# A channel-attention kernel: part of x kept on the chip in 12 bits an element

## The chip, the cores and the metric

The kernel runs on one core of one Trainium2 chip. The metric is the device time of a launch in microseconds (us): the median of several executions. One execution was also taken by the hardware profiler; its span, from the first to the last instruction, is what the views of the profile divide up.

## The reference

x is 384 x 384 pixels by 384 channels in bf16 (147,456 pixels, 113.2 MB). For each channel the mean and the maximum over all pixels are computed, both go through the same small two-layer network, and a sigmoid of the sum scales the channel:

```python
B, H, W, C = x.shape
xf = x.reshape(B, H * W, C)
gap = jnp.mean(xf, 1)
gmp = jnp.amax(xf, 1)
h_a = gap @ w1
h_a = h_a * (h_a > 0)
h_m = gmp @ w1
h_m = h_m * (h_m > 0)
scale = _sigmoid(h_a @ w2 + h_m @ w2)
return x * scale[:, None, None, :]
```

The elements of x are normal numbers times 0.05 in bf16. No output can be written before all of x was read once, and x is far larger than the memory on the chip.

## The kernel before, in words

The pixels are cut into 1152 "rows": a row is 128 pixels, one on each partition, times 384 channels, 98,304 bytes in all. A block of n rows gives each partition n neighbouring pixels, so a transfer of a block has one run of n x 768 bytes for each partition. Six slots of 44 rows (`SLOTS`), a buffer `held` of 21 rows and an accumulator `acc` of 11 rows lie in SBUF; 16 + 2 rows are kept in PSUM (`kept_ps`, `kept_b`).

**Pass 1** goes over the list `loads` (lines 137 to 207). Each load is issued from SP's queue (line 184). TensorE sums its rows over the partitions with matmuls by a vector of ones (`sums`, line 157; four rows at a time, and the three groups of 128 channels write to partitions 0, 32 and 64 of one PSUM bank); the last loads are summed by `tail_sums` (line 174). VectorE keeps the running maximum in `acc` (line 200), in instructions over 6 and 5 rows in turn. The first 16 + 2 rows are copied to PSUM (lines 205 and 207). A load into a slot waits until VectorE and TensorE have done with what lay there. The blocks of `PASSING` go through the slots and are forgotten; those of `STAYING` come last and stay.

**The turn** (lines 210 to 241): `turn_sums` and `tail_sums` end the means, the 11 rows of `acc` are folded to one, three transposes and reductions end the maxima, and small matmuls and a sigmoid give `scale_bc`, the scale on all partitions. The 11 rows that `acc` displaced are read again.

**Pass 2** multiplies on VectorE (line 246) and stores from ACT's queue (line 264). `put` multiplies and stores a block in pieces, `get` reads a block again into a slot whose last store has landed (SP's queue, line 273). The order of SP is the order written in the loop; `FIRST_STORES` and `FIRST_READS` cut the first blocks in pieces, and the first two slots are read into after both were put (`LEAD`). 838 rows are read again (`AGAIN`). At the end come `held` and the rows kept in PSUM, which are multiplied into a slot:

```python
    while k < len(order):
        put(order[k], stores.pop(0) if stores else (order[k][1],), None if k else ACC_STORES_AT)
        k += 1
        if k == LEAD:
            for j in range(k):
                read_into(order[j][2])
        elif k > LEAD:
            read_into(order[k - 1][2])
```

Tile, the layer below, sets the semaphores by the regions that instructions read and write, and orders the engines by its own plan except where `manual_schedule` names an engine.

Of the kernel before, what the change touches and what calls it, by code (L numbers as in the profile page):

```python
# [13 lines left out]
U32 = mybir.dt.uint32  # L14


SLOTS = (44, 44, 44, 44, 44, 44)
PSUM_ROWS = 16
RING_BYTES = 256
HELD_ROWS = 21  # L20
BANK_ROWS = 2

FIRST_LOAD = 4
ACC_PARTS = ((0, 6), (6, 11))
ACC_ROWS = 11

PASSING = (
    43, 44, 44, 43, 43, 44, 43, 42, 42, 39, 38, 37, 36, 36, 35, 34, 32, 29, 29, 27, 27, 23, 15, 13,
)
STAYING = (  # L30
    (19, 17, 8), (18, 16, 10), (16, 14, 14), (13, 11, 11, 9), (10, 9, 9, 8, 8), (6, 6, 5, 5, 5, 4, 4, 3, 3, 3),
)

AGAIN = (44,) * 18 + (23, 23)

FIRST_STORES = ((1, 2, 3, 4, 4, 6, 8, 8, 8), (8, 8, 9, 9, 10), (10, 12, 22))

FIRST_READS = ((8, 8, 8, 10, 10), (44,))
LEAD = 2

ACC_STORES_AT = 3
SUM_TAIL = 4
# [4 lines left out]
def kernel(  # L47
# [15 lines left out]
    NS = len(SLOTS)  # L63
# [5 lines left out]
    def rows_of(ap, first, n):  # L69

        return ap[first * P:(first + n) * P, :].rearrange("(p n) c -> p n c", n=n)
# [4 lines left out]


    beside = BANK_ROWS + A
    held_at = PSUM_ROWS + beside
    head = held_at + HELD_ROWS  # L80
    n_stay = sum(SLOTS)
    n_pass = TOT - head - n_stay
    assert sum(PASSING) == n_pass
    stay = []
    for i, n in enumerate(SLOTS):
        stay.append([head + n_pass + sum(SLOTS[:i]), n, i])
    assert sum(AGAIN) == n_pass
    again = [(head + sum(AGAIN[:i]), n) for i, n in enumerate(AGAIN)]

# [8 lines left out]
    NQP = (CQ - 1) * QP + 1  # L98
    pick = small[0:NQP, 10:10 + 2 * CQ].bitcast(F32)
    nc.vector.memset(pick, 0.0)  # L100
    for q in range(CQ):
# [12 lines left out]
    acc = consts.tile([P, A, C], BF16)  # L114
    nc.dynamic_dma_scratch_size = RING_BYTES
    nc.lookup_mloc("DynamicDMAScratchLoc").dims = [P, RING_BYTES]
    held = nc.alloc_sbuf_tensor_at("held", [P, HELD_ROWS, C], BF16, offset=RING_BYTES).ap()
    slots = [xpool.tile([P, n, C], BF16, name=f"x{s}") for s, n in enumerate(SLOTS)]

# [4 lines left out]
    sum_ps = bank_a[0:NQP, 0:MM_ROWS * P]  # L124
    nc.vector.memset(bank_a, 0.0)
    tp_ps = [
# [10 lines left out]

    bufs = [*slots, held]
    loads = [
        (0, PSUM_ROWS, NS - 2, 0, PSUM_ROWS), (PSUM_ROWS, beside, NS - 1, 0, beside), (held_at, HELD_ROWS, NS, 0, HELD_ROWS),  # L140
    ]
    done = head
    for i, n in enumerate(PASSING):
        loads.append((done, n, (i - len(PASSING)) % NS, 0, n))
        done += n
    for (first, n, s), pieces in zip(stay, STAYING):
        assert sum(pieces) == n
        for j, m in enumerate(pieces):
            loads.append((first, n, s, sum(pieces[:j]), sum(pieces[:j + 1])))
    n_loads = len(loads)  # L150
    tail_rows = sum(hi - lo for *_, lo, hi in loads[n_loads - SUM_TAIL:])
# [13 lines left out]
    def turn_sums():  # L165

        for r in range(MM_ROWS):
            nc.scalar.copy(out=s_sb[r % 2], in_=sum_ps[:, r * P:(r + 1) * P])  # L168
            nc.tensor.matmul(gsum_ps, lhsT=s_sb[r % 2], rhs=pick, start=(r == 0), stop=False)  # L169
# [9 lines left out]
    done = turn = 0  # L179
    for i, (first, n, s, lo, hi) in enumerate(loads):  # L180
        rows = bufs[s][:, lo:hi, :]
        m = hi - lo
        for a, b in ((0, FIRST_LOAD), (FIRST_LOAD, m)) if i == 0 else ((0, m),):
            nc.sync.dma_start(out=rows[:, a:b, :], in_=rows_of(xr, first, n)[:, lo + a:lo + b, :])  # L184
        if i < n_loads - SUM_TAIL:
            sums(rows, m, done, TOT - tail_rows)
        else:
            tail_sums(rows, m, i == n_loads - 1)
        done += m
        if i == n_loads - SUM_TAIL - 1:  # L190
            turn_sums()
        if i == 0:
            nc.vector.tensor_copy(out=acc, in_=rows[:, 0:A, :])  # L193
            lo = A
        j = 0 if i else A
        while j < m:
            c, e = ACC_PARTS[turn]
            turn = (turn + 1) % len(ACC_PARTS)
            e = min(e, c + m - j)
            nc.vector.tensor_tensor(  # L200
                out=acc[:, c:e, :], in0=acc[:, c:e, :], in1=rows[:, j:j + e - c, :], op=ALU.max
            )
            j += e - c
        if i == 0:
            nc.vector.tensor_copy(out=kept_ps.bitcast(U32), in_=rows.bitcast(U32))  # L205
        elif i == 1:
            nc.vector.tensor_copy(out=kept_b.bitcast(U32), in_=rows[:, 0:BANK_ROWS, :].bitcast(U32))

# [7 lines left out]
    def acc_rows(ap, lo, hi):  # L216
        return rows_of(ap, PSUM_ROWS, beside)[:, BANK_ROWS + lo:BANK_ROWS + hi, :]

    n = A
    acc_pieces = []  # L220
    while n > 1:
        h = n // 2
        nc.vector.tensor_tensor(out=acc[:, 0:h, :], in0=acc[:, 0:h, :], in1=acc[:, n - h:n, :], op=ALU.max)  # L223
# [4 lines left out]
        nc.sync.dma_start(out=acc[:, lo:hi, :], in_=acc_rows(xr, lo, hi))  # L228
        acc_pieces.append((lo, hi))
    for q0, part in tp_ps:  # L230
        n = part.shape[1]
        for q in range(q0, q0 + n):
            nc.tensor.transpose(out=part[:, q - q0, :], in_=acc[:, 0, q * P:(q + 1) * P], identity=ident_bf)  # L233
        nc.vector.tensor_reduce(out=gT[:, q0:q0 + n, 1], in_=part, axis=AX.X, op=ALU.max)  # L234
# [105 lines left out]
```

## Time and profile before

| | |
|---|---|
| median of 3 runs | 737.08 us (736.64 to 741.11) |
| profiled execution: time, span | 737.92 us, 736.1 us |
| TensorE busy, mean granted clock | 128.1 us (17%), 0.554 |
| VectorE busy | 490.2 us (67%) |
| ScalarE, GpSimd busy | 3.3 us, 0.7 us |
| moved | 310.26 MB: 196.85 read, 113.25 written; 421 GB/s over the span |
| first load issued, first multiply of pass 2, last multiply | 0.7, 275.8, 697.9 us |

In the views, PE is TensorE's matmuls and PEld its weight loads, DVE is VectorE, ACT ScalarE, SP the engine that issues the loads. The slices cut the span in 40 parts and give the busy share of each engine in tenths, and the rate of the transfers. A line of the groups names the line of the kernel, the engine, the operation and the shapes, then the busy time of the group, the mean time of one in ns, and the idle time in front of them with what ended it.

### The profile page before, as it was taken

What the parts mean: (1) busy time and instruction counts of PE and PEld (TensorE: products, weight loads), DVE (VectorE), ACT (ScalarE), POOL (GpSimd) and SP (SyncE); (2) the same over time, 40 slices, a digit from 0 to 9 for tenths busy, and PEclk for the clock granted to TensorE, in tenths of its full rate; (3) what the DMA queues carried; (4) which work ended last, traced back from release to release, by engine and by line L of the source; (5) the groups of instructions that cost most, each with busy time, mean ns of one, the idle gap of its engine ahead of it and who ended that gap; (6) DMA issues with size and microseconds to landing.
All of it is one profiled execution on the core that took longest, in us unless ns stands there. A gap on an engine that the chain in (4) does not pass through costs nothing.

```text
span 736.1 us, 2598 instructions
## 1 busy us (share of the span) xinstructions
PE 128.1 (17%) x969; PEld 41.1 (6%) x969; DVE 490.2 (67%) x286; ACT 3.3 (0%) x9; POOL 0.7 (0%) x6
## 2 busy tenths in 40 slices
PE   3334454454544550000000000000000000000000
PEld 0111111111111120000000000000000000000000
DVE  6789999999999989999444464444444444445400
ACT  0000000000000000000000000000000000000000
POOL 0000000000000000000000000000000000000000
PEclk9856667655556555555555555555555555555555
DMA  9999999999999979999999999999999999999998
GB/s 382 438 431 435 423 433 423 431 426 431 423 427 418 417 277 370 415 423 438 425 435 439 432 428 435 437 433 428 435 437 433 428 435 437 433 424 436 436 428 346
DMA packets 18956, 310.26 MB, mean 421 GB/s; under 512 B 2464, under 2 KB 3072, under 8 KB 8320
## 3 DMA queue, kind: packets, MB, share of 16 engines
q1 hardware_dynamic: 12464, 196.86, 63.0%
q10 hardware_dynamic: 6480, 113.25, 36.1%
q8 instruction: 7, 0.11, 0.1%
q14 instruction: 5, 0.04, 0.0%
HBM read 196.85 MB, written 113.25 MB: 421 GB/s over the span
## 4 chain that ended last, share of the span: by engine, by line
another core or an unknown queue 39%; DMA 39%; DVE 13%; DVEq 1%; SPq 1%; issue 1%; PE 0%; ACT 0%; ACTq 0%
DMA x<-in_x_dram 32%; DVE acc L200 10%; DMA out_dram<-x 7%; DVE x L246 2%; DVEq L335 1%; SPq L273 1%; SPq L184 0%; DVE acc L223 0%; DVE acc L246 0%; PE bank_a L240 0%; ACT scale_bc L241 0%; DVE small L234 0%; PE bank_a L233 0%; PE bank_a L238 0%
## 5 line engine op out<-in xcount | busy, mean ns | idle before, releaser
L246 DVE TENSOR_TENSOR x<-x,scale_bc 128x16896 bf16<-128x16896 bf16 (+11 forms) x40 | 224.9, 5665 | 188.6 <-DMA x<-in_x_dram 187.4
L200 DVE TENSOR_TENSOR acc<-acc,x 128x2304 bf16<-128x2304 bf16 (+5 forms) x221 | 241.4, 1167 | 12.6 <-DMA x<-in_x_dram 12.3
L157 PE MATMUL bank_a<-x,small 128*1 128x512 bf16 (+3 forms) x894 | 120.9, 571 | 140.4 <-DMA x<-in_x_dram 140.4
L157 PEld LDWEIGHTS <-small 128*1 128x1 bf16 x912 | 37.1, 110 | 229.2 <-issue 226.5
L193 DVE COPY acc<-x 128x4224 bf16<-128x4224 bf16 x1 | 1.3, 1260 | 5.2 <-DMA x<-in_x_dram 5.2
L200 DVE TENSOR_TENSOR acc<-acc,held 128x2304 bf16<-128x2304 bf16 (+2 forms) x4 | 4.6, 1201 | 0.0
L246 DVE TENSOR_TENSOR held<-held,scale_bc 128x8064 bf16<-128x8064 bf16 x1 | 4.4, 4351 | 0.0
L205 DVE COPY kept_ps<-x 128x3072 uint32<-128x3072 uint32 x1 | 3.4, 3355 | 0.0
L246 DVE TENSOR_TENSOR x<-kept_ps,scale_bc 128x6144 bf16<-128x6144 bf16 x1 | 3.4, 3350 | 0.0
L157 PE MATMUL bank_a<-held,small 128*1 128x512 bf16 (+1 forms) x18 | 2.4, 570 | 3.2 <-DMA held<-in_x_dram 3.2
L223 DVE TENSOR_TENSOR acc<-acc 128x384 bf16<-128x384 bf16 (+2 forms) x4 | 2.6, 658 | 0.1
L246 DVE TENSOR_TENSOR acc<-acc,scale_bc 128x1920 bf16<-128x1920 bf16 (+1 forms) x2 | 2.4, 1252 | 0.0
L168 ACT COPY w_sb<-bank_a 65x128 f32<-65x128 f32 x2 | 0.5, 262 | 265.2 <-PE bank_a L157 264.7
L174 PEld LDWEIGHTS <-x 128*128 128x128 bf16 x39 | 1.3, 109 | 0.0
L113 ACT ACT_TABLE_LOAD x1 | 1.3, 1283 | 0.7 <-PEq L324 0.7
L169 PE MATMUL bank_b<-small,w_sb 65*128 65x3 f32 x4 | 1.2, 365 | 0.4 <-ACT w_sb L168 0.4
L174 PE MATMUL bank_b<-small,x 128*128 128x1 bf16 x39 | 1.2, 165 | 0.0
L169 PE MATMUL bank_b<-small,scale_bc 65*128 65x3 f32 x4 | 1.1, 353 | 0.0
L169 PEld LDWEIGHTS bank_b<-small,w_sb 65*128 65x128 f32 x4 | 1.0, 313 | 0.9 <-ACT w_sb L168 0.9
L169 PEld LDWEIGHTS bank_b<-small,scale_bc 65*128 65x128 f32 x4 | 1.1, 323 | 0.0
L234 DVE TENSOR_REDUCE small<-bank_a 128x2 bf16<-128x256 bf16 x1 | 0.4, 427 | 0.6 <-PE bank_b L233 0.6
L233 PE MATMUL bank_a<-ident_bf,acc 128*128 128x128 bf16 x2 | 0.4, 301 | 1.9 <-DVE acc L223 1.9
(27 smaller groups left out, 7.5 us busy)
## 6 DMA issues: line engine op xcount, KB each, us to landing
out_dram<-x ACTq DMA_DIRECT2D x21, 4224.0 KB, 79.7
x<-in_x_dram SPq DMA_DIRECT2D x20, 4224.0 KB, 27.7
x<-in_x_dram SPq DMA_DIRECT2D x4, 4128.0 KB, 51.6
x<-in_x_dram SPq DMA_DIRECT2D x2, 4032.0 KB, 50.0
x<-in_x_dram SPq DMA_DIRECT2D x2, 3456.0 KB, 44.1
x<-in_x_dram SPq DMA_DIRECT2D x3, 2208.0 KB, 23.0
x<-in_x_dram SPq DMA_DIRECT2D x2, 2784.0 KB, 38.1
x<-in_x_dram SPq DMA_DIRECT2D x2, 2592.0 KB, 35.5
```

Source lines behind the costliest of these rows:

```text
L113: nc.scalar.activation(out=scale_bc[0:1, 0:1], in_=pick[0:1, 0:1], func=ACT.Sigmoid)
L157: nc.tensor.matmul(sum_ps[q * QP:q * QP + 1, 0:g * P], lhsT=ones_bf[:, 0:1], rhs=rows[:, k:k + g, q * P:(q + 1) * P], start=(done + k == 0 ...
L168: nc.scalar.copy(out=s_sb[r % 2], in_=sum_ps[:, r * P:(r + 1) * P])
L169: nc.tensor.matmul(gsum_ps, lhsT=s_sb[r % 2], rhs=pick, start=(r == 0), stop=False)
L174: nc.tensor.matmul(gsum_ps[:, q:q + 1], lhsT=rows[:, k, q * P:(q + 1) * P], rhs=ones_bf, start=False, stop=(last and k == n - 1 and q == C ...
L193: nc.vector.tensor_copy(out=acc, in_=rows[:, 0:A, :])
L200: nc.vector.tensor_tensor(out=acc[:, c:e, :], in0=acc[:, c:e, :], in1=rows[:, j:j + e - c, :], op=ALU.max)
L205: nc.vector.tensor_copy(out=kept_ps.bitcast(U32), in_=rows.bitcast(U32))
L223: nc.vector.tensor_tensor(out=acc[:, 0:h, :], in0=acc[:, 0:h, :], in1=acc[:, n - h:n, :], op=ALU.max)
L246: nc.vector.tensor_tensor(out=dst, in0=src, in1=scale_bc.unsqueeze(1).to_broadcast([P, n, C]), op=ALU.mult)
L273: nc.sync.dma_start(out=slots[s][:, j:j + m, :], in_=rows_of(xr, first, n)[:, j:j + m, :])
L335: with _tile.TileContext(nc) as tc:
```

## The change

Three of the six slots go. In their place 18 blocks of 44 rows (`packed_b`) pass through the slots in pass 1, and the last 8 rows of each stay in 6 rows of room (`planes`): the low bytes as they are (4 rows), and four bits of each high byte (its top bit, the sign, and its three lowest), four elements to a 16-bit code (2 rows). ScalarE splits the bytes and takes the sign of the last two rows, TensorE adds four high bytes with the weights 256, 16, 1 and 4096 and the sign with two more into one exact number, ScalarE writes it as uint16 (`pack`). This holds only where the other four bits of the high byte are 0111; VectorE takes the difference from that (`look`), TensorE sums it over partitions and blocks (`look_sums`), and at the end every engine loads the sum and branches: where it isn't zero, the 144 rows are read, multiplied and stored again. In pass 2 such a block is read without its last 8 rows (36 rows), and `unpack` rebuilds them: a byte copy on ScalarE, five bit fields and two ORs on VectorE.

The maxima run over 22 rows an instruction until the last packed, plain and open blocks are through, then over 11; the first load of 22 rows goes straight into that accumulator. 24 rows of room beside it (`spare`) are loaded late and stay, as does the buffer of 21 rows (`hole`), which holds the work space of the packing before. The orders of ACT and VectorE in pass 2 are now those of the code, and the two held buffers are put before the last two blocks.

The core of the diff:

```diff
-SLOTS = (44, 44, 44, 44, 44, 44)
+SLOT = 44
+NS = 3
+PACKED = 8
+GROUP = 4
+N_PACK = 18
+HIGH = 0x3800
+HIGH_MASK = 0x7800
+WEIGHTS = (256.0, 16.0, 1.0, 4096.0, 262144.0, -4.0)
+ACC_ROWS = 11
+WIDE = 22
+SPARE_ROWS = 24
+OPEN_ROWS = 55
+PLAIN_ROWS = (44, 44, 22)
+HALVES = (22, 22)
+PLAIN = ((22, 22), (19, 11, 14), (14, 8))
+OPEN_PIECES = (12, 11, 10)
+HELD_PIECES = ((21,), (13, 11))
-STAYING = (
-    (19, 17, 8), (18, 16, 10), (16, 14, 14), (13, 11, 11, 9), (10, 9, 9, 8, 8), (6, 6, 5, 5, 5, 4, 4, 3, 3, 3),
-)
+STAYING = ((22, 22), (11, 11, 11, 11), (11, 11, 9, 7, 6))
-SUM_TAIL = 4
+SUM_TAIL = 2
...
+    def pack(k, rows):
+        low, code = planes(k)
+        halves = rows.bitcast(U8).rearrange("p n (c t) -> p n c t", t=2)
+        nc.scalar.copy(out=high, in_=halves[:, :, :, 1])
+        nc.scalar.activation(out=sign, in_=rows[:, PACKED - n_grp:PACKED, :], func=ACT.Sign)
+        nc.scalar.copy(out=low, in_=halves[:, :, :, 0])
+        for w in range(len(WEIGHTS)):
+            for g in range(n_grp):
+                src = high[:, w * n_grp + g, :] if w < GROUP else sign[:, g, :]
+                nc.tensor.matmul(
+                    pack_ps[g], lhsT=diag[:, w, :], rhs=src, start=(w == 0), stop=(w == len(WEIGHTS) - 1)
+                )
+        for g in range(n_grp):
+            nc.scalar.activation(out=code[:, g, :], in_=pack_ps[g], func=ACT.Copy, bias=-OFFSET)
+
+    def look(k, rows):
+        nc.vector.tensor_scalar(
+            out=odd.bitcast(U16), in0=rows.bitcast(U16), scalar1=HIGH, scalar2=HIGH_MASK,
+            op0=ALU.bitwise_xor, op1=ALU.bitwise_and,
+        )
+
+    def look_sums(k):
+        flat = odd.rearrange("p n c -> p (n c)")
+        n = PACKED * C // 512
+        for c in range(n):
+            nc.tensor.matmul(
+                odd_ps, lhsT=ones_bf[:, 0:1], rhs=flat[:, c * 512:(c + 1) * 512],
+                start=(k == 0 and c == 0), stop=(k == N_PACK - 1 and c == n - 1),
+            )
...
+        nc.sync.dma_start(out=rows, in_=part(xr, block, lo, hi))
...
+        if looked is not None:
+            look_sums(looked)
+            looked = None
...
+        if i == n_wide:
+            larger(acc, acc, wide[:, A:WIDE, :])
+            width = A
+        for j in range(0, m, width):
+            e = min(width, m - j)
+            larger(store[:, 0:e, :], store[:, 0:e, :], rows[:, j:j + e, :])
+        if k is not None:
+            look(k, rows[:, m - PACKED:m, :])
+            pack(k, rows[:, m - PACKED:m, :])
+            looked = k
...
+    def unpack(item):
...
+        nc.scalar.activation(out=rows, in_=low, func=ACT.Copy, bias=float(HIGH))
...
+        for r in range(GROUP - 1):
+            field(bits[:, r * n_grp:(r + 1) * n_grp, :], 4 * r, ALU.logical_shift_left, HIGH_BITS)
+        last = bits[:, PACKED - n_grp:PACKED, :]
+        field(more, 12, ALU.logical_shift_left, 0x8000)
+        field(last, 4, ALU.logical_shift_right, 0x0700)
+        add(last, last, more)
+        add(rows, rows, bits)
...
+    in_order.enter_context(tc.manual_schedule(engines={
+        mybir.EngineType.SP, mybir.EngineType.Activation, mybir.EngineType.DVE}))
...
+        elif k > LEAD:
+            read_into(s)
+        if 1 < k and k - 2 + NS < len(order):
+            unpack(order[k - 2 + NS])
+        if k == last - 2:
+            put_held()
...
+    odd_one = nc.values_load(
+        flag.bitcast(U32), min_val=0, max_val=2**31 - 1, skip_runtime_bounds_check_because="any value will do"
+    )
+    with tc.If(odd_one != 0):
+        for k, b in enumerate(packed_b):
+            rows = slots[k % NS][:, SLOT - PACKED:SLOT, :]
+            nc.sync.dma_start(out=rows, in_=part(xr, b, SLOT - PACKED, SLOT))
+            multiply(rows, rows)
+            nc.scalar.dma_start(out=part(orr, b, SLOT - PACKED, SLOT), in_=rows)
```

## The prediction

> **What bounds the kernel now.** I read the page's slices first, then the chain that ended last, the groups by form, and the stretches around the turn between the two passes.
>
> ```profile
> DVE  6789999999999989999444464444444444445400
> DMA  9999999999999979999999999999999999999998
> GB/s 382 438 431 435 423 433 423 431 426 431 423 427 418 417 277 370 415 423 438 425 435 439 432 428 435 437 433 428 435 437 433 428 435 437 433 424 436 436 428 346
> ```
>
> The transfers fill every slice but the fifteenth (about 276 us), where the sums and maxima become the scale. VectorE fills nine tenths too, but only in the first pass. In the second pass the chain repeats itself:
>
> ```profile
> 392.53 19.56 another core or an unknown queue
> 412.47 19.56 another core or an unknown queue
> 432.44 19.55 another core or an unknown queue
> ```
>
> Each 19.94 us reads 44 rows (a row is 128 partitions x 384 bf16, 98,304 B) and writes 44: 8.65 MB, or 434 GB/s, **0.2266 us a row**. All 310.26 MB at that rate would take 715 us of the 736.1 us span. So a row that isn't moved is worth 0.2266 us wherever nothing else becomes the bound. The other candidate is VectorE in pass 1:
>
> ```profile
> L246 DVE TENSOR_TENSOR x<-x,scale_bc 128x16896 bf16<-128x16896 bf16 x21 | 187.8, 8957 | 170.6 <-DMA x<-in_x_dram 170.6
> L200 DVE TENSOR_TENSOR acc<-acc,x 128x2304 bf16<-128x2304 bf16 x93 | 125.9, 1354 | 11.7 <-DMA x<-in_x_dram 11.5
> L205 DVE COPY kept_ps<-x 128x3072 uint32<-128x3072 uint32 x1 | 3.4, 3355 | 0.0
> L193 DVE COPY acc<-x 128x4224 bf16<-128x4224 bf16 x1 | 1.3, 1260 | 5.2 <-DMA x<-in_x_dram 5.2
> L241 ACT ACTIVATE scale_bc<-bank_a 128x384 bf16<-128x384 f32 x1 | 0.5, 491 | 3.9 <-PE bank_a L240 3.9
> L212 ACT ACTIVATE small<-bank_b 128x3 bf16<-128x3 f32 x1 | 0.2, 177 | 1.7 <-PE bank_b L174 1.7
> ```
>
> From the first two: (8957 - 1354) / (16896 - 2304) = 0.521 ns an element, 154 ns fixed. On the page the 225 maxima of line 200 are busy 241.4 + 4.6 = 246.0 us for 1141 rows (228.3 us at 0.521 ns), so in a row each instruction adds only 17.7 / 225 = 79 ns. The copy of line 193 runs at 0.262 ns an element, that of line 205 at 1.042.
>
> **What the change removes: traffic.** Kept before: 264 rows in slots + 21 + 18 in PSUM (the 11 rows under acc are read again) = 303 of 1152. Kept after: 3 x 44 + 21 + 24 spare + 18 + 18 x 8 packed = 339. Reads fall by **36 rows, 36 x 0.2266 = 8.2 us**, not by 144 rows: the packed rows take 108 rows of room and three slots are given up for them. Writes are the same.
>
> **VectorE in pass 1.** Maxima: 1130 rows of loads + 11 folded at the narrowing = 228.3 us, now in 68 instructions instead of 225: + 5.4 = 233.7 us, 12.3 less. Added: 18 `look` instructions over 3072 uint16 elements, one source, two bit operations, which the trace doesn't hold. Bounds: line 193's rate, 0.80 + 0.08 = 0.88 us, 15.9 us in all; line 205's rate, 3.28 us, 59 us in all. I take the first: like line 193 it reads and writes 2-byte elements in SBUF, while line 205 has 4 bytes and PSUM. With the PSUM copies (as before, 4 us) VectorE has 233.7 + 15.9 + 4.1 = 254 us against 251 before (246.0 + 3.9 + 1.3). Transfers of the pass need 1152 x 0.2266 = 261 us. In a packed block of 44 rows that is 8.96 + 0.88 = 9.84 us against 9.97: it fits, barely. After the last packed block 324 rows follow at 0.204 to 0.207 us a row, so a lag shrinks by about 7 us. Before, VectorE worked without a break from 231 us to the end of the pass:
>
> ```profile
> 255.00:260.00 5.00, 3.17 (x21) 0.80 (x21) 4.91 (x6) 0.00 (x0) 0.00 (x0) 0.50 1.02 409
> 266.00:268.00 2.00, 1.36 (x7) 0.85 (x6) 2.00 (x3) 0.57 (x3) 0.00 (x0) 0.50 0.82 308
> 268.00:270.00 2.00, 2.00 (x42) 1.99 (x42) 2.00 (x4) 0.38 (x2) 0.00 (x0) 0.50 0.22 75
> ```
>
> (PE, PEld, DVE, ACT, POOL busy, clock, DMA share, GB/s.) Loads end at 268.5, maxima at 270.3; pieces of 3 to 6 rows moved at 400 to 409 GB/s. After: first data as before (16 rows had landed at 6.8, so the origin is 3.2), the last landing at 3.2 + 261 = 264 at best, 268.5 at the mean 427 GB/s of 20 to 260 us; then 6 rows of maxima, 1.35 us: 265.5 to 270. I take 268.3, **2 us gained**, bounds 0 to 5. From there to the first store the code is the same (2.7 us of folds, 2.7 to the scale).
>
> **ScalarE and TensorE in pass 1.** ScalarE was idle, so this is hidden while it fits 9.97 us a block. Slope from lines 241 and 212: (491 - 177) / 381 = 0.82 ns, so two byte planes of 3072 take 2.7 us each, the sign (768) 0.8, two codes 0.49 each: 7.2 us. By proportion to line 241 alone (1.28 ns) it would be 9.8, still inside. TensorE gets 12 matmuls of 384 columns and 6 of 512 a block, beside 33 of 512 (in threes, side by side):
>
> ```profile
> 104.57 4.65 PE L157 MATMUL bank_a<-x,small 128*1 128x512 bf16 x33 [4.92 <-DMA x<-in_x_dram]
> 113.46 3.81 PE L157 MATMUL bank_a<-x,small 128*1 128x512 bf16 x30 [4.25 <-DMA x<-in_x_dram]
> 116.73 0.30 PEld L157 LDWEIGHTS <-small 128*1 128x1 bf16 x4 [0.19 <-issue]
> ```
>
> A triple takes 4.65 / 11 = 0.42 us. At that pace: 4.65 + 12 x 0.32 + 6 x 0.42 + 12 weight loads of 0.11 = 12.3 us, more than 9.97. But the second burst's late triples come closer (3.81 / 10 = 0.38 on average, the last spacing 0.33): longer bursts run faster, and a queue that falls behind has no gaps. At twice the pace it is some 7 us. I cost it at nothing; if that cover is gone, it is rival 3. [...]
>
> **Pass 2 with three slots.** Period: 36 + 44 rows = 80 x 0.2266 = 18.1 us. Block j's slot is that of block j-3. On ACT's queue `unpack` of block j+1 stands between the stores of blocks j-1 and j, and its byte copy waits for the store of j-2 to land; on VectorE the multiply of j stands behind that block's final OR. So after landing of j-2: 2.7 (copy) + 1.75 (OR over 3072) + 8.96 (multiply) = 13.4 us, then the store of j is queued. The five bit fields and the small OR (0.3 to 0.55 us each at the fast rates) run ahead of the wait. Meanwhile the store of j-1 (44 rows) and the read of j+1 (36 rows, SP, free at the same landing) are 18.1 us of transfer: 4.7 us to spare. With every unpack operation at 1.042 ns VectorE has 8.96 + 9.0 = 18.0 us a block, still just inside. Nothing added. At the entrance 44 + 11 + 44 rows of stores and 36 of read are queued when the first unpack holds VectorE 4 to 5 us: covered too. `put_held` moves 45 rows of stores ahead of the last two blocks, so they still overlap reads.
>
> **The test.** Every engine loads a word from SBUF and branches. Before, the last multiply ended at 698.5 and stores drained for 37 us; if the load and branch lie there they cost 0. If the block boundary waits for the last store, it costs two meetings like the one at the end (735.4 to 736.1, 0.7 us each) and up to two fetches like w1's 2.0 us (issue 268.8, use 270.8): 5.4. I take **2 us**. [...]
>
> **Sum.** -8.2 - 2 + 2 = -8.2 us. The profiled execution took 737.92 (span 736.1); its own sum is 729.7, and the median of the runs lies 0.8 lower: **729.0**. Bounds within this case: 724 (gain of 5 at the turn, test hidden) to 735 (no gain there, test 5.4, some 2.6 lost at the entrance).
>
> **Rivals.** (1) `look` runs at two elements a cycle, like the maxima: 1.68 us, 18 x 0.8 = 14.4 us more, of which some 7 is recovered or waited anyway: 736.5. For: it is a new operation; against: line 193. (2) Slower: **look at one element a cycle**. A packed block then costs VectorE 12.2 us against 9.97; VectorE's sum is 297 us from about 9, so the pass ends near 305 instead of 270. 737.1 - 8.2 + 34.5 + 2 = 765. It decides from 1.0 us a look on. For: the bit operations; against: the 2-byte copy. (3) TensorE stays at 0.42 us a triple: 2.4 us x 18 = 43 us of lag. About 20 us of it is covered by the loads queued in the other two slots and is caught up in the last 324 rows; 23 stalls the loads: 754. Against: its own faster late triples. (4) Three slots leave gaps in pass 2: if the chain of 13.4 us is really above 18.1, each us beyond costs 20 us over the blocks; at 19 it is 749. For: four steps in a row on three engines; against: the 4.7 us. (5) The second way is taken: 288 more rows, 65 us. In the given inputs every magnitude lies between 0x3980 and 0x3e14, inside the tested field, so 0.
>
> **Chances.** Forecast 0.56, rivals 0.09, 0.14, 0.12, 0.09, 0. A measurement tells about 1% (7.4 us) from nothing. The forecast lies near that edge: 0.37 faster, 0.19 within. Rival 1 is within but for 0.02; rival 4 is slower but for 0.02. Faster 0.37, same 0.28, slower 0.35. The range 724 to 762 leaves out most of rival 2 (0.10), the worst of 3 and 4 (0.04) and a little below. The forecast's own: 724 to 735.
>
> **What would show it.** Right: `look` near 0.9 us, DMA slices full through both passes, 306.7 MB, a period near 18.1 us, pass 1 over before 270. Wrong: `look` at 1.7 or 3.3; SP's loads waiting on PE or ACT; VectorE waiting on ScalarE in pass 2 while DMA slices show 8 or less; more than 3 us between the last landing and the end.

## The result, and the profile after

The changed kernel takes a median of 741.41 us (737.17 to 744.94, 15 runs), the kernel before 736.79 (736.27 to 741.11, 15 runs beside them): ratio of the means 1.0048, 95% interval 1.0027 to 1.0069. It is half a per cent slower; the forecast was 729.0, a gain of eight us. Its executions scatter over 5 us and more, the kernel before mostly over 2, so single profiles are read below for where time goes, and medians for how much. The profiled execution took 741.41, span 739.6 (before 736.1).

The slices of the kernel after:

```profile
DVE  5899999999999998897766666666666665444850
PEclk9878898888865555555555555555555555555555
DMA  9999999999999958999999999999999999999996
GB/s 380 421 429 427 426 426 426 427 428 427 424 421 426 420 235 318 393 438 429 423 438 433 428 427 439 433 425 440 436 427 427 431 433 429 407 428 435 426 440 264
```

The transfers are still full but for the turn. That dent is deeper (235 and 318 GB/s in the fifteenth and sixteenth slices; 277 and 370 before), and the last slice is emptier (264 for 346). Three groups by form:

```profile
L252 DVE TENSOR_TENSOR store<-store,x 128x8448 bf16<-128x8448 bf16 x37 | 168.5, 4555 | 6.9 <-DMA x<-in_x_dram 6.4
L405 DVE TENSOR_TENSOR x<-x,store 128x3072 uint16<-128x3072 uint16 x18 | 31.6, 1758 | 91.9 <-ACT x L399 91.9
L271 DVE TENSOR_SCALAR held<-x 128x3072 uint16<-128x3072 uint16 x18 | 17.1, 952 | 0.0
```

A `look` (line 271) takes 952 ns and the OR of `unpack` (line 405) 1.76 us, as forecast. The first line holds the 22-row maxima: 4.555 us for 4.40 us of rows. Next the two windows in the middle of the passes, kernel before and then after (columns: length; busy time of PE, PEld, DVE, ACT, POOL; clock; DMA share; GB/s):

```profile
20.00:190.00 170.00, 77.17 (x573) 23.80 (x575) 158.16 (x141) 0.00 (x0) 0.00 (x0) 0.64 1.00 430
420.00:650.00 230.00, 0.00 (x0) 0.00 (x0) 111.61 (x13) 0.00 (x0) 0.00 (x0) 0.50 1.00 433
```

```profile
20.00:190.00 170.00, 112.54 (x903) 45.86 (x905) 165.27 (x51) 116.72 (x83) 0.00 (x0) 0.84 1.01 426
420.00:650.00 230.00, 0.00 (x0) 0.00 (x0) 150.16 (x90) 30.38 (x11) 0.00 (x0) 0.50 1.01 430
```

The transfers never stop, and are 1% slower in both passes. At the turn VectorE's timeline gives (start, length, work; kernel before and then after):

```profile
231.73 38.56 DVE L200 TENSOR_TENSOR acc<-acc,x 128x2304 bf16<-128x2304 bf16 x39 [0.18 <-DMA x<-in_x_dram]
270.32 2.74 DVE L223 TENSOR_TENSOR acc<-acc 128x1920 bf16<-128x1920 bf16 x4
275.82 1.50 DVE L246 TENSOR_TENSOR x<-x,scale_bc 128x384 bf16<-128x384 bf16 x3 [1.17 <-ACT scale_bc L241]
```

```profile
201.88 0.70 DVE L315 TENSOR_REDUCE small<-bank_a 1x1 f32<-1x512 f32 x1 [1.55 <-PE bank_a L280]
202.61 30.50 DVE L252 TENSOR_TENSOR store<-store,x 128x8448 bf16<-128x8448 bf16 x10
...
276.48 2.74 DVE L252 TENSOR_TENSOR store<-store 128x1920 bf16<-128x1920 bf16 x4
279.78 0.43 DVE L348 TENSOR_REDUCE small<-bank_a 128x2 bf16<-128x256 bf16 x1 [0.56 <-PE bank_b L347]
...
281.98 1.50 DVE L360 TENSOR_TENSOR x<-x,scale_bc 128x384 bf16<-128x384 bf16 x3 [1.17 <-ACT scale_bc L355]
```

The folds begin at 276.5 instead of 270.3, and the first multiply comes at 282.0 instead of 275.8: **6.2 us later**. From there to the end the kernel after takes 457.6 us and the kernel before 460.3: only **2.7 us less**. At its end, the windows show:

```profile
726.00:728.00 2.00, 0.00 (x0) 0.00 (x0) 0.00 (x0) 0.00 (x0) 0.00 (x0) 0.50 1.02 439
728.00:730.00 2.00, 0.00 (x0) 0.00 (x0) 0.00 (x0) 0.00 (x0) 0.00 (x0) 0.50 0.28 118
730.00:732.00 2.00, 0.00 (x0) 0.00 (x0) 0.00 (x0) 0.00 (x0) 0.00 (x0) 0.50 0.06 25
732.00:734.00 2.00, 0.00 (x0) 0.00 (x0) 0.00 (x0) 0.00 (x0) 0.00 (x0) 0.50 0.26 111
734.00:736.00 2.00, 0.00 (x0) 0.00 (x0) 0.00 (x0) 0.00 (x0) 0.00 (x0) 0.50 1.06 442
```

```profile
716.55 0.55 DVE L360 TENSOR_TENSOR x<-bank_b,scale_bc 128x768 bf16<-128x768 bf16 x1
732.86 0.34 ACTq L460 DMA_DIRECT2D out_dram<-x  x1
```

The last multiply ends at 717.1, but the store of its 18 rows (line 460) is issued at 732.9, when all other transfers have landed: the build put it behind the branch of the test, and the side that is taken here waits for the transfers first. Five us of transfer time stay empty.

Three terms are thus to be explained: the turn, the end, and the reads.

### The profile page after: what moved, and what is told of

Its sections match the earlier page's. It is cut to its first block, busy times and chain, and to the rows that moved or that the text cites. A ratio compares the mean times of both kernels' runs of the same rounds, so it can differ in the third digit from the quotient of the medians.

```text
span 739.6 us, 3511 instructions
## 1 busy us (share of the span) xinstructions
PE 165.0 (22%) x1320; PEld 64.3 (9%) x1320; DVE 562.8 (76%) x277; ACT 179.5 (24%) x123; POOL 0.7 (0%) x6
## 2 busy tenths in 40 slices
DMA packets 20113, 306.79 MB, mean 415 GB/s; under 512 B 2592, under 2 KB 3072, under 8 KB 6784
## 4 chain that ended last, share of the span: by engine, by line
DMA 61%; DVE 27%; ACT 6%; issue 1%; PE 0%; SPq 0%; DVEq 0%; ACTq 0%
DMA x<-in_x_dram 34%; DMA out_dram<-x 28%; DVE x L360 14%; DVE store L252 11%; ACT x L399 2%; ACT held L257 2%; ACT store L259 2%; DVE x L405 1%; ACT held L258 1%; DVE store L360 0%; DVE kept_ps L318 0%; PE bank_a L280 0%; DVE store L402 0%; SPq L289 0%; DVEq L464 0%
## 5 line engine op out<-in xcount | busy, mean ns | idle before, releaser
L360 DVE TENSOR_TENSOR x<-x,scale_bc 128x16896 bf16<-128x16896 bf16 (+10 forms) x39 | 220.5, 5682 | 42.5 <-DMA x<-in_x_dram 41.3
L252 DVE TENSOR_TENSOR store<-store,x 128x8448 bf16<-128x8448 bf16 (+11 forms) x63 | 226.8, 3600 | 15.5 <-DMA x<-in_x_dram 14.3
L399 ACT ACTIVATE x<-store 128x3072 uint16<-128x3072 uint8 x18 | 49.7, 2762 | 282.0 <-DMA out_dram<-x 248.1
L230 PE MATMUL bank_a<-x,small 128*1 128x512 bf16 (+2 forms) x882 | 88.0, 440 | 74.8 <-DMA x<-in_x_dram 73.6
L405 DVE TENSOR_TENSOR x<-x,store 128x3072 uint16<-128x3072 uint16 x18 | 31.6, 1758 | 91.9 <-ACT x L399 91.9
L257 ACT CAST held<-x 128x3072 bf16<-128x3072 uint8 x18 | 49.5, 2752 | 70.8 <-DMA x<-in_x_dram 70.8
L263 PE MATMUL bank_b<-held 128*128 128x384 bf16 x108 | 46.3, 429 | 21.7 <-ACT held L257 21.7
L259 ACT COPY store<-x 128x3072 uint8<-128x3072 uint8 x18 | 49.2, 2736 | 0.0
L263 PE MATMUL kept_ps<-held 128*128 128x384 bf16 x108 | 45.9, 426 | 0.0
L280 PE MATMUL bank_a<-held,small 128*1 128x512 bf16 x108 | 27.5, 392 | 0.4 <-DVE held L271 0.4
L252 DVE TENSOR_TENSOR store<-store 128x4224 bf16<-128x4224 bf16 (+4 forms) x8 | 10.3, 1282 | 0.2
```

What stands on the lines that cost most here:

```text
L230: nc.tensor.matmul(sum_ps[q * QP:q * QP + 1, 0:g * P], lhsT=ones_bf[:, 0:1], rhs=rows[:, k:k + g, q * P:(q + 1) * P], start=(done + k == 0 ...
L252: nc.vector.tensor_tensor(out=out, in0=a, in1=b, op=ALU.max)
L257: nc.scalar.copy(out=high, in_=halves[:, :, :, 1])
L259: nc.scalar.copy(out=low, in_=halves[:, :, :, 0])
L263: nc.tensor.matmul(pack_ps[g], lhsT=diag[:, w, :], rhs=src, start=(w == 0), stop=(w == len(WEIGHTS) - 1))
L280: nc.tensor.matmul(odd_ps, lhsT=ones_bf[:, 0:1], rhs=flat[:, c * 512:(c + 1) * 512], start=(k == 0 and c == 0), stop=(k == N_PACK - 1 and ...
```

## The experiments

Ratios are to the kernel before, run beside each. Turn is the first multiply, pass 2 the time from it to the end, both in the one profiled execution (after: 282.0 and 457.6). The fifteen traces that read 36 rows of a packed block and store it whole have a pass 2 of 452.4 to 457.9 us, whatever was edited, so two traces don't tell a difference of 2 us there from nothing. The kernel before has one trace.

### The test

**e1**: the flag is copied once more behind the last multiply and the branch reads the copy, which leaves the last store ahead of the branch.

```diff
+    flag_late = small[FLAG:FLAG + 1, 12:14]
...
+    nc.vector.tensor_copy(out=flag_late, in_=flag)
     odd_one = nc.values_load(
-        flag.bitcast(U32), ...
+        flag_late.bitcast(U32), ...
```

> The word that the engines load and branch on is copied once more on VectorE behind the last multiply, so that the store of the last 18 rows is issued ahead of the branch. Theory (the last store waited, behind the branch, for every other transfer: issued at 732.9 though its multiply ended at 717.1, and some 5 us of transfer time stood empty between 728 and 734): the last store goes out near 717 and the whole is 4 to 6 us shorter than the changed kernel, about 736. Rival (the load and the branch themselves cost the time, or the drain of the last stores takes as long in any order): no change, 741.

741.24 us, ratio 1.0053 (1.0040 to 1.0066); turn 283.0, pass 2 456.2. The store is now issued at 717.8 and the hole is gone, but the end is no earlier by its length:

```profile
730.00:732.00 2.00, 0.00 (x0) 0.00 (x0) 0.00 (x0) 0.00 (x0) 0.00 (x0) 0.50 1.01 433
732.00:734.00 2.00, 0.00 (x0) 0.00 (x0) 0.00 (x0) 0.00 (x0) 0.00 (x0) 0.50 0.60 257
734.00:736.00 2.00, 0.00 (x0) 0.00 (x0) 0.00 (x0) 0.00 (x0) 0.00 (x0) 0.50 0.05 21
736.00:738.00 2.00, 0.00 (x0) 0.00 (x0) 0.00 (x0) 0.00 (x0) 0.00 (x0) 0.50 0.03 14
```

From 734 on a share of 0.05 and 0.03 is one of sixteen transfer engines, still at work 3.7 us after the median one has done. Before, that tail was 2.1 us. Pass 2 is 1.4 us shorter, not 4 to 6, and that is within the spread of the traces. The time from the start of the last multiply of 44 rows to the end leaves out the reads before it: it is 44.6 to 44.7 us in five of the six traces with 36-row reads and the store behind the branch (43.3 in e8), and 43.5 to 44.5 in the seven with the store ahead. The store left behind costs about 1 us.

**e2**: no load of the flag, no branch, no second way (the flag itself is still computed).

```diff
-    odd_one = nc.values_load(flag.bitcast(U32), ...)
-    with tc.If(odd_one != 0):
-        ...
```

> Leaves out the load of the word, the branch and the second way; the test's sums stay. Theory: the same gain as with the store ahead of the branch, 4 to 6 us, and no more than 1 us beyond it, as the branch itself lies beside the drain of the stores. Rival (the branch itself is dear): 3 us or more below the kernel with the store ahead.

739.72 us, 1.0009 (0.9989 to 1.0029); turn 283.7, pass 2 455.6: 2.0 us less in pass 2. From the start of the last multiply of 44 rows to the end it takes 43.1 us, in e4 43.9: beside the 43.5 to 44.5 with the store ahead, the load and the branch themselves can't be made out.

**e3**: the reduction of the flag on VectorE (0.70 us, after a wait of 1.55 for TensorE's sums of the last `look`) two loads later.

```diff
-                nc.vector.tensor_reduce(out=flag.bitcast(F32), in_=odd_ps, ...)
+                reduce_at = i + 2
...
+        if i == reduce_at:
+            nc.vector.tensor_reduce(out=flag.bitcast(F32), in_=odd_ps, ...)
```

> The reduction of the test's sums on VectorE is emitted two loads later, behind the maxima that are ready. Theory (VectorE stood 1.55 us for TensorE's sums and 0.7 for the reduction at 201 us, never caught up, and ended the maxima 7.8 us after the last landing): the turn comes 1.5 to 2 us earlier, 739.5. Rival (the lag at the end of the pass is made by the pieces after it, whatever happened at 201 us): no change in the turn, 741.

739.72 us, 1.0021 (1.0007 to 1.0035); turn 280.7, pass 2 457.6. The wait was on the path, and all of it arrives at the turn. It differs between executions: 1.55 to 3.16 us in the eight traces that have the reduction in this place and the packed blocks' 22-row loads and maxima (after, e1, e2, e6, e7, e10, e11, e14), and in each the first multiply comes at 280.4 to 280.7 us plus the wait. The longest is that of e2, whose turn is 283.7:

```profile
203.60 0.70 DVE L315 TENSOR_REDUCE small<-bank_a 1x1 f32<-1x512 f32 x1 [3.16 <-PE bank_a L280]
```

e3 and e5 have no such wait, and turns of 280.7 and 280.5.

**e4**: no test at all, neither `look`, its sums, the reduction nor the branch.

```diff
-            look(k, rows[:, m - PACKED:m, :])
...
-            looked = k
-            if k == N_PACK - 1:
-                ...
```

> Leaves out the whole test: look, its sums, the reduction, the branch and the second way. Theory: the gain at the end (5) and at the turn (2 from the reduction, 1 from the last look) together: 733. If the looks were what made VectorE late all through pass 1, more than 10 us: 731 or less. If the lag comes from the pieces at the end of the pass, only the 5 us at the end: 736.

737.59 us, 0.9996 (0.9985 to 1.0007); turn 280.0, pass 2 455.9. All of the test costs 3.8 us of median; by the two profiles it is 2.0 in the turn, of which 1.55 is the wait of e3, and 1.7 in pass 2. VectorE is rid of 17 us of `look`, and still the turn is 4.2 us later than before: the sum of VectorE's work isn't what makes it late.

**e5**: e1 and e3 together.

> The last store ahead of the branch and the reduction two loads later, together. Theory: the two gains are in different places and add: the first multiply of pass 2 near 280.7 (as with the reduction alone), pass 2 about 456 long (as with the store alone), span 736.5 to 737.5, some 2 to 3 us under the changed kernel's 739.6. Rival (one transfer engine that lags at the end of both passes sets both ends, whatever is moved): 739 or more.

738.29 us, 1.0017 (1.0000 to 1.0033); turn 280.5, pass 2 455.7. The two edits win back 3.1 of the 3.8 us and keep the test.

### The reads of 36 rows

**e6**: all 44 rows of a packed block are read again, and `unpack` does nothing. The packing, the test and three slots stay.

```diff
-        j = block[1] if k is None else block[1] - PACKED
+        j = block[1]
...
     def unpack(item):
+        return
...
```

> Pass 2 reads the packed blocks whole (44 rows) and leaves the rebuilding out; packing and test stay in pass 1. This undoes the saved traffic and the unpacking together, with the three slots left: 144 rows more. Theory (pass 2 is bound by transfers, three slots are enough): a period of 20.0 us a block, as before the change with six slots, and 739.6 + 144 x 0.2266 = 772. Rival (three slots or the unpacking already cost time in pass 2): a period of 20.3 or more if it is the slots; 768 to 770 if it is the unpacking that this leaves out.

770.38 us, 1.0465 (1.0442 to 1.0488); turn 282.7, pass 2 485.8, a period of 19.96 us as before. So **three slots cost nothing**. But 144 rows more cost 485.8 - 457.6 = 28.2 us, not 144 x 0.2266 = 32.6: in the profile of the kernel after, the blocks of 36 rows are some 4.4 us slower than their bytes. That isn't so in every execution: e15 below reads the same 36 rows, and against its pass 2 of 452.4 us the 144 rows cost 33.4 (about 1 of it is e15's store ahead of the branch).

**e7**: 36 rows are read, nothing is rebuilt (so the last 8 rows of a packed block are not those of x).

```diff
     def unpack(item):
+        return
```

> Leaves the rebuilding out: 36 rows are read, the last 8 rows of a packed block are multiplied and stored as the slot's last tenant left them. Theory (the chain copy, OR, multiply has some 4 us to spare): the period stays at 18.3 us, the total within 1.5 us of the changed kernel. Rival (the period is 18.3 and not 18.1 because of that chain): 18.1, 3 to 4 us shorter.

741.81 us, 1.0058 (1.0040 to 1.0075); pass 2 457.9, median period 18.48 (18.38 after). `unpack` costs nothing; the slower blocks are a matter of the transfers. There the trace shows this (times by packet, which here is one partition's run): the median packet of 33,792 B takes 1251 ns and that of 27,648 B 1025 ns, in every kernel that moves them. That is the same time a byte within 0.2%, so between these two the length by itself costs nothing (the 234 ns of 6,144 B are 3% more a byte). But some packets are held up, by 0.1 to 1.2 us. Counting those of these two sizes over 60 ns late from 290 us on, the kernel before has 35, none of them after 360 us, e6 has one, and the kernel after 120, with 40.8 us in all. The engines fall out of step: from 600 to 690 us the first and the last of a transfer end 6 to 8 us apart, in e6 never more than 3.

The number differs between executions of the same reads. Behind 360 us the kernel after has 92 packets held up, e3 122, but e13 20, e17 14 and e15 6. Those three have the shortest pass 2, 454.2, 453.2 and 452.4 us. The middle of pass 2 in e15, beside 430 GB/s after and 433 before:

```profile
420.00:650.00 230.00, 0.00 (x0) 0.00 (x0) 148.37 (x88) 30.39 (x11) 0.00 (x0) 0.50 1.00 433
```

Its median period is 18.17 us, against 18.1 forecast. So reads of 36 rows can move as fast as forecast; what makes one execution hold many packets up and another few is open.

**e10**: e6, with each 44-row read as two of 22.

```diff
-        get(item, reads.pop(0) if reads else (rows_read(b, k),))
+        n = rows_read(b, k)
+        get(item, reads.pop(0) if reads else (n // 2, n - n // 2))
```

> The kernel that reads all 44 rows of each packed block again and rebuilds nothing (e6), with each such read of pass 2 as two transfers of 22 rows. Nothing is skipped between the rows that it reads, but its packets (16,896 B) are unlike those of the stores (33,792 B). Theory (packets of unlike sizes in the two queues put the sixteen transfer engines out of step, and packets get held up): as in the kernel after, 60 to 120 packets of pass 2 take over 60 ns longer than the usual time of their size, the engines of one transfer end 6 us or more apart, and pass 2 takes 489 to 491 us instead of 485.8; time 773 to 776. Rival (the 8 rows skipped in each 44 of the kernel after do it, through the addresses that they leave out): no more than five such packets, the engines within 3 us, 771 (two packets of 629 ns for one of 1251 cost 1 us over the blocks).

780.18 us, 1.0582 (1.0548 to 1.0616); pass 2 496.3, 316 packets held up, by 115 us in all. The slices of e6 and then of e10:

```profile
GB/s 383 420 428 427 428 424 425 431 423 428 422 425 422 408 147 376 445 427 427 445 422 436 436 427 445 422 436 436 426 445 424 436 434 427 445 424 434 434 430 321
```

```profile
GB/s 380 423 428 426 428 429 422 428 428 425 423 424 421 344 225 380 430 432 432 430 435 425 439 390 438 410 428 430 422 429 416 424 426 412 432 424 424 418 434 279
```

The same bytes in the same order move 10 us slower, twice what the theory asked for, with dips to 390 and 410. No row is skipped here, so the addresses that the 36-row reads leave out are not needed for it: packets shorter than the stores' are enough, or twice as many transfers, which this edit also makes.

**e11**: the kernel after with the store of a packed block as 36 and 8 rows, so that most packets of the two queues are alike.

```diff
-            nc.scalar.dma_start(out=part(orr, block, j, j + m), in_=rows)
+            cut = m - PACKED if item[2] is not None and m == SLOT else m
+            nc.scalar.dma_start(out=part(orr, block, j, j + cut), in_=rows[:, 0:cut, :])
+            if cut < m:
+                nc.scalar.dma_start(out=part(orr, block, j + cut, j + m), in_=rows[:, cut:m, :])
```

> The changed kernel with the store of a packed block as two transfers, of 36 and of 8 rows, so that the packets of the long stores are like those of the 36-row reads (27,648 B). Theory (unlike sizes): packets held up fall from 120 to under 30, the engines stay within 4 us, pass 2 shrinks from 457.6 by 2 to 4 us less 1 us for the added packets (some 8 ns each, 8 an engine a block): time 738 to 740. Rival (the skipped addresses of the reads, or any read shorter than 44 rows): as many held up as before, time 741 to 743.

745.73 us, 1.0102 (1.0047 to 1.0158); pass 2 463.4, 340 packets held up, by 124 us. A miss: making the long packets alike does not cure it, and the added short ones make it worse. The engines are in step here (from 600 to 690 us the first and the last of a transfer end 0.4 to 1.8 us apart), so being out of step isn't needed for the loss. What in an engine holds a packet up stays open; behind 360 us the traces have 0 (before) and 1 (e6) where both queues carry 44-row runs, 6 to 122 with 36-row reads, and 295 and 316 with a shorter kind added (e11, e10).

### The turn

**e8**: packed blocks loaded whole instead of in halves of 22 rows.

```diff
-HALVES = (22, 22)
+HALVES = (44,)
```

> The packed blocks are loaded in one transfer of 44 rows instead of two of 22. Theory (runs of 16.9 KB a partition instead of 33.8 are why loads moved at 426 GB/s and not at the 430 of the kernel before): 430 between 20 and 190 us, the last landing 1.5 us earlier, but maxima start later in each block, so the total gains at most 1 us. Rival (loads are slowed by something else, such as the wait for the packing before a slot is free): 426 or less, and with a coarser wait a slower pass.

741.24 us, 1.0060 (1.0045 to 1.0076). Loads run at 430.6 GB/s between 20 and 190 us (426 after, 430 before) and the last one lands at 270.5 (271.8 after, 269.4 before): the 22-row runs cost the landings 1.3 us. The turn is later all the same, 283.7, and VectorE doesn't wait for the flag's sums here, as it doesn't in e3 and e5 (280.7 and 280.5): it is some 3 us further behind. That it gets 44 rows at a time is the likely reason.

**e9**: 11-row maxima from the start.

```diff
-        if i == n_wide:
+        if i == 1:
```

> Undoes the 22 rows of maxima alone: the accumulator is narrowed to 11 rows ahead of the packed blocks, so a packed block of 44 rows costs VectorE four maxima of 2.36 to 2.39 us and a look of 0.95, 10.4 to 10.5 us, against the 10.05 to 10.1 us in which its rows land. Theory (VectorE sets the turn): it falls 0.35 to 0.45 us behind in each of 18 blocks, 6 to 8 us; the narrowing fold of 2.36 us leaves the end of the pass, and some 140 later rows cost 1.3 us more. First multiply at 286 to 289 us instead of 282.0, time 745 to 748. Rival (the late landing sets the turn and VectorE only follows it): first multiply stays at 281 to 283, time 740 to 742.

740.63 us, 1.0036 (1.0017 to 1.0055); turn 283.2. A miss: four maxima and a `look` take 10.3 us a block against 10.1 of landings, so VectorE falls behind by 0.2 us a block and not by 0.4; and being late it no longer waits for the flag's sums, and has no narrowing near the end. Against e3 and e5, which don't wait for the sums either, the 22-row maxima are worth 2.6 to 2.8 us at the turn.

**e12**: e5, with the copies of the five late rows into PSUM (0.75 and 0.55 us) on ScalarE.

```diff
-                nc.vector.tensor_copy(out=kept_ps[:, 0:LATE_ROWS, :].bitcast(U32), in_=...)
-                nc.vector.tensor_copy(out=kept_b.bitcast(U32), in_=...)
+                nc.scalar.copy(out=kept_ps[:, 0:LATE_ROWS, :].bitcast(F32), in_=...)
+                nc.scalar.copy(out=kept_b.bitcast(F32), in_=...)
```

> The kernel with the last store ahead of the branch and the reduction two loads later (e5), and the two copies of the five late rows into PSUM (0.75 and 0.55 us on VectorE) done by ScalarE, which has nothing to do there. Theory (the turn is set by VectorE's unbroken work behind the last packed block): all 1.3 us arrive at the turn, first multiply at 279.0 to 279.4 instead of 280.5, and the median of e5, 738.3, falls to 736.5 to 737.5: level with the kernel before. Rival (the last landing at 271.7 and its straggling transfer engine set the turn): first multiply stays at 280 to 281, time 738 to 739.

(Two bf16 elements go as one f32 number here; that this keeps every value is not shown.) 737.78 us, 0.9992 (0.9973 to 1.0011); turn 280.3, only 0.1 earlier. The timeline says why: with the 1.3 us gone VectorE meets its loads.

```profile
235.63 4.75 DVE L253 TENSOR_TENSOR store<-store,x 128x4224 bf16<-128x4224 bf16 x2 [0.27 <-DMA x<-in_x_dram]
240.68 4.75 DVE L253 TENSOR_TENSOR store<-store,x 128x4224 bf16<-128x4224 bf16 x2 [0.30 <-DMA x<-in_x_dram]
```

**e13 and e14**: the loads of that place (22 and 21 rows) in halves, on e12 and on the kernel after.

```diff
-HELD_PIECES = ((21,), (13, 11))
-STAYING = ((22, 22), (11, 11, 11, 11), (11, 11, 9, 7, 6))
+HELD_PIECES = ((11, 10), (13, 11))
+STAYING = ((22, 11, 11), (11, 11, 11, 11), (11, 11, 9, 7, 6))
```

> The kernel with the late copies on ScalarE (e12), with the 22 rows before the held ones loaded as 11 and 11 and the 21 held rows as 11 and 10; VectorE's instructions are the same in number and size. In e12 VectorE waits for loads until 246 us and from there is behind by one load's maxima (4.55 us for 21 rows), which it cannot make good at 0.22 us a row. Theory (the size of these loads sets the turn): VectorE starts on them 2.3 us earlier, until it meets the last landing at 271.7 to 272 plus six rows of maxima (1.36 us); first multiply at 278.6 to 279.2 instead of 280.3, median 736.2 to 737.2, under the kernel before by 0.1 to 0.2%. Rival (the number of VectorE's instructions behind 246 us, not the landings, sets it): 280 to 280.6 and 737.5 to 738.5.

> The changed kernel with the same edit of load sizes alone. Theory: VectorE there works without a break from 195 us, behind its loads, so smaller loads change nothing until the lag is gone: first multiply 281.6 to 282.6 (282.0 in the kernel after), time 741 to 742. Rival (the size of these loads acts by itself): first multiply 280 to 280.8, time 739.5 to 740.5.

e13: 737.90 us, 0.9996 (0.9980 to 1.0012), turn 280.0; e14: 741.41 us, 1.0050 (1.0032 to 1.0068), turn 283.2 (280.7 without its wait of 2.54 us for the flag's sums, 280.4 after). Smaller loads bring nothing at either place. In e13 the rival's figures hold, but what counts is less the number of VectorE's instructions than what each costs. From 235.59 VectorE works for 38.94 us without a wait, on 177 rows in 18 maxima. The line of before at 231.73 above is 176 rows in 39 maxima, in 38.56 us. At 0.2 us a row the first has 197 ns for each instruction beyond its rows, the second 86.

**e15 and e17**: e13, with each 22-row maximum as two of 11 rows, on the two halves of the 22 accumulated rows in turn (e17 is e15 timed).

```diff
-        for j in range(0, m, width):
-            e = min(width, m - j)
-            larger(store[:, 0:e, :], store[:, 0:e, :], rows[:, j:j + e, :])
+        for j in range(0, m, A):
+            e = min(A, m - j)
+            o = j % width
+            larger(store[:, o:o + e, :], store[:, o:o + e, :], rows[:, j:j + e, :])
```

> The kernel with the small late loads (e13), with each 22-row maximum as two of 11 rows, on the upper and the lower half of the 22 accumulated rows in turn. Theory (a maximum in a row costs 0.08 to 0.09 us beyond its rows when the one before wrote other rows, 0.18 to 0.20 when it wrote the same): in the packed blocks, where a 22-row load is two maxima in turn, the second starts 2.28 to 2.29 us behind the first (2.38 behind one another in the kernel with narrow maxima, e9); behind the narrowing to 11 rows it is still 2.38. Rival (the cost in a row belongs to the length of the instruction, not to what it follows): 2.38 in both places. The time is expected to be that of e13 (737.9), since two such maxima take 4.58 us and one of 22 rows 4.56 to 4.58.

> The kernel with 11-row maxima in turn (e15) once more, timed. It does what the kernel with small late loads (e13, 737.9) does in the same time on VectorE, so the theory has its median at 737.0 to 738.2, and its single 734.4 as the low end of a scatter of 5 us. Rival (the order of the maxima shifts more than VectorE's time): 734 to 736, under the kernel before by 0.2 to 0.4%.

Four maxima of 11 rows: e15 in a packed block, e15 behind the narrowing, then a packed block of e9.

```profile
190.39 9.32 DVE L253 TENSOR_TENSOR store<-store,x 128x4224 bf16<-128x4224 bf16 x4
235.69 9.54 DVE L253 TENSOR_TENSOR store<-store,x 128x4224 bf16<-128x4224 bf16 x4 [0.44 <-DMA x<-in_x_dram]
```

```profile
191.69 9.53 DVE L252 TENSOR_TENSOR store<-store,x 128x4224 bf16<-128x4224 bf16 x4
```

The first line has a pause of 0.08 us before its third maximum, which begins another load. One by one, an 11-row maximum of e15 starts 2.27 us behind one that went to the other half, and 2.39 behind one on the same rows (2.39 throughout a block of e9). Its rows are 2.20: **0.07 us against 0.19**. e17: 736.99 us, 0.9998 (0.9980 to 1.0015), turn 280.1; e15's single 734.4 was scatter.

**e16**: e15, with the maxima behind the narrowing over 6 and 5 rows in turn, as in the kernel before.

```diff
+            parts = ((0, A), (A, WIDE)) if width == WIDE else ((0, 6), (6, A))
+            o, end = parts[turn % 2]
+            turn += 1
...
-STAYING = ((22, 11, 11), (11, 11, 11, 11), (11, 11, 9, 7, 6))
+STAYING = ((22, 11, 11), (11, 11, 11, 11), (11, 11, 11, 6, 5))
```

> The kernel with 11-row maxima in turn (e15), in which the maxima behind the narrowing run over 6 and 5 rows in turn as in the kernel before, and the last loads are 11, 11, 11, 6 and 5 rows. Theory (0.07 us for a maximum in a row on other rows, 0.19 on the same): 177 rows in some 33 instructions take 35.4 + 33 x 0.07 = 37.7 us instead of 38.9, so the turn comes about 1 us earlier, first multiply at 278.9 to 279.4 (280.1 in e15); median 736.3 to 737.3. Rival (the landings and their latest transfer engine set the turn by now): 279.8 to 280.4, median as e17.

736.05 us, 0.9981 (0.9965 to 0.9998); turn 279.6. The last maxima take 38.4 us in 34 instructions, with short waits for loads up to 269 us: half of the expected us, for by now VectorE meets the landings. It is the one version whose interval lies under the kernel before, by 0.2% in the middle and ending just short of 1; as one of seventeen runs, that is hardly a gain shown. Against the kernel after its median is 5 us lower.

## Why the prediction was wrong

The forecast was -8.2 for the reads, -2 for the turn, +2 for the test: -8.2 in sum. The profiles give +6.2 for the turn and -2.7 for pass 2, where the reads and the end of the test lie together: +3.5 in sum (739.6 - 736.1). Of the 11.7 us between the two sums, 8.2 lie in the turn. That 741.41 falls in the range of 724 to 762 is luck: its upper part was there for rivals 2 to 4.

- **"36 x 0.2266 = 8.2 us" came in only in part.** Bytes and price are right: 306.79 MB, transfers full, no gap, and in e15 pass 2 is 7.9 us shorter than before. What the step left out is that packets were held up where the reads are shorter than the stores. In the profile of the kernel after, 92 are, behind 360 us, the middle of pass 2 runs at 430 GB/s instead of 433, and only 2.7 us are left, with about 1 us lost to the late store. Why one execution has many and another few is open.
- **The turn went the other way, and this made the kernel slower.** Two steps failed. "264 at best, 268.5 at the mean" has the last landing too early. It came at 271.8, 2.4 later than before (269.4; the prediction read 268.5 from the windows). 1.3 of that is the 22-row runs (e8); about the rest goes with the transfer engine that lands last, 1.9 us behind the median one, before 0.5. And "324 rows follow at 0.204 to 0.207 us a row, so a lag shrinks by about 7 us": the maxima ended 4.7 us behind the last landing instead of 0.9. The step assumed 79 ns for an instruction in a row, read from maxima that alternate between two parts of `acc`. The change sends them all to the same rows, where it is 0.19 us (e15), so that half as many instructions bought nothing, and the last 177 rows ran at 0.220 us a row. The copies and the narrowing then lay in a stretch that had no slack for them, and so did the reduction's wait for TensorE (1.55 us, e3), which the sum left out.
- **The test, 2 us**, cost about 1 at the end by the time behind the last multiply, 1.7 by e4's pass 2. That is near what was taken, but by luck: neither the load nor the branch was seen to cost it, but the last store left behind the branch, and a trailing engine that hides most of that hole (e1). In the profile of the kernel after, the five branch instructions (line 467) took 45 to 211 ns; no run shows the two fetches of 2.0 us that the bound of 5.4 counts. What the forecast missed is its 2.0 us in the turn.
- **Right**: `look` at 0.95 us (0.88 forecast), which ends rivals 1 and 2 (two elements a cycle and one stand there for the measured 0.521 and 1.042 ns an element; no view shows a cycle); ScalarE's 2.75, 2.74 and 0.84 us; TensorE, whose 512-column matmuls fell from 597 to 464 ns on average while the clock between 20 and 190 us rose from 0.64 to 0.84 (rival 3); three slots and `unpack` at nothing (rival 4; e6, e7); no second way. TensorE was busy for 112.5 of those 170 us instead of 77.2, or 6.7 us for each packed block of 10.1 us, against "some 7 us" at "twice the pace", a factor that was the author's estimate. The two bursts of the prediction, of 33 matmuls in 4.65 us and 30 in 3.81, don't show that longer bursts run faster.
- **Two sums of the prediction don't come out**, which changes nothing above: the terms named for the upper bound of 735 give 736.9 (737.1 - 8.2 + 5.4 + 2.6), and rival 4 at a period of 19 us gives 747 by its own price, not 749.

None of the rivals was the true case. The one that was missing: a stretch ahead of the turn in which VectorE has no slack for any of the small things added there, and packets of pass 2 held up, in some executions more than in others.

## What to carry to other kernels

Read the price of a removed transfer from more than one execution: with the same reads pass 2 was 2.7 us shorter than before in one trace and 7.9 in another, and the late store is only about 1 us of that difference. Where one engine sets the end of a stage, look at what each of its instructions follows: two accumulators in turn cost 0.07 us an instruction, one accumulator 0.19, and longer instructions may only pay that back. And a test that does nothing still has an end: see that no store is left behind its branch.

## What the runs showed of the hardware

- A maximum on VectorE that updates the rows which the one before it has just written started 0.12 us later than one that goes to other rows (2.39 and 2.27 us behind it, for 11 rows each; e15). So what an 11-row maximum costs beyond its rows was 0.07 or 0.19 us, by which rows the one before it wrote, and for the last 177 rows 34 short maxima in turn (38.4 us; e16) beat 18 long ones (38.9; e13).
- One transfer engine of sixteen fell 6 to 8 us behind over pass 2, with the transfers all at full share (after, share 1.01 from 420 to 650 us; in e15, with the same reads, 1.2 us). The trace doesn't name the engine of a packet, but packets can be followed from the end of one to the start of the next. In e5 one engine so moved 9.65 MB from 320 to 680 us where the others moved 9.70 to 9.73, by longer times of its packets, hardly by pauses (the longest was 0.1 us). A wait for a whole transfer then ends with that engine: at the end of e5 it lands 3.4 us behind the median one.
- Packets were hardly ever held up where reads and stores are all 44 rows (before from 360 us on none, e6 one), and 6 to 122 times with reads of 36. Splitting the 44-row reads in two gave 316 and cost 10 us of pass 2 (e10).
